# Block-causal attention and a feed-forward on one core: V loaded in f32 and cast on GpSimd, weights in pieces, a full last key block, and attention of batch b placed among the feed-forward of batch b-2

## The chip, the cores and the metric

The kernel runs on one core of a Trainium2 chip. A core has TensorE (PE in the profile; PEld is its weight load), VectorE (DVE), ScalarE (ACT), GpSimd (POOL) and SyncE (SP), each with an instruction stream of its own that runs in the order in which it was written; they meet through semaphores. Sixteen DMA engines move data between HBM and SBUF. The metric is the device time of one execution in microseconds (us); lower is better.

## The reference

Eight batches of eight heads, 576 positions of 64 elements. Attention is block-causal in blocks of 64, and its output, with the heads side by side, is the input of a feed-forward with the gate h * sigmoid(beta * h):

```python
scores = np.matmul(q, k.transpose(0, 1, 3, 2)) / np.sqrt(64)     # (8, 8, 576, 576)
scores = np.where(block_i >= block_j, scores, -1e9)              # block = position // 64
attn = np.exp(scores - scores.max(-1)); attn /= attn.sum(-1) + 1e-9
x = np.matmul(attn, v).transpose(0, 2, 1, 3).reshape(4608, 512)
h = x @ w_in                                                     # 512 -> 2048
g = h * (1.0 / (1.0 + np.exp(-beta * h)))
out = g @ w_out                                                  # 2048 -> 512, float32
```

## The kernel before

**Attention units.** The work of attention is cut into 32 units u = 4b + c, one for batch b and head pair c. Each unit goes through these steps:

- Q and K of the pair are loaded in f32 by one DMA each on SP (L396) into one of four buffers, and cast to bf16 (L402), on DVE for units 0 to 3 and on POOL after that.
- PE transposes them, six matmuls each (L408); DVE copies the result to QT and KT (L416).
- PE makes the scores in four groups g0 (L437). The contraction is over 64 rows, and the two heads of the pair use the two halves of the array. ACT takes the exponential of the three large groups (L444) into E and of the last key block, 64 keys, into F (L456). POOL clears the masked corners of E (L450, L452).
- AV (L482): for each head and each block i of 128 queries, PE multiplies the key blocks t = 0 to i of E by V, 15 matmuls a head, 30 a unit. V has a column of ones as its 65th, so the sum of the exponentials comes out beside the product. Query block 4 has only 64 queries and key block 4 only 64 keys, so its weights are 64 columns wide, and for t = 4 the contraction is over 64 rows: head h lies in rows 64h to 64h + 63 of F and of V's fifth block.
- DVE takes the reciprocal of the sums (L493) and multiplies (L501); PE transposes the result (L510), and DVE copies it into xT (L516), the input of the feed-forward.

V of a batch is loaded by six DMAs on POOL (L370, L374), which cast to bf16 on the way, into one of two buffers Vn; batch 0 in two halves of four heads.

**Feed-forward chunks.** Nine chunks r of 512 rows. First half: for j = 0 to 15, four matmuls with w_in (L531), tanh on ACT (L539) and the product on DVE into gT (L543; the sigmoid is written through tanh, with the factor one half applied to beta and to the output). Second half: for w = 0 to 3, sixteen matmuls with w_out (L551), a copy with the factor one half (L560) on ACT or DVE, and the store on SP (L566). Chunk r needs the attention of every batch that its rows touch: chunk 0 needs batch 0, chunk 1 batches 0 and 1.

**Weights.** w_in and w_out are loaded on POOL with a cast to bf16, in four operations of four DMAs each (L345, L351).

**What sets the order.** Every operation is entered in a planner (`Plan`, L40) with the engines that may run it, an assumed duration and latency, its dependencies, the buffers ("tiles") that it needs, and a priority `prio`. `schedule` (L68) plays the program through with these numbers. Whenever an engine is free it takes the ready operation with the lowest prio, and for a tile the slot that is free. The result is a fixed order on each engine, written out by `emit` (L246) with semaphore waits in front of each operation. At run time the order doesn't change: an operation that waits holds all that stand behind it on its engine. PSUM has eight banks; 0 to 3 serve the scores in pairs (class "PP") while scores are still to come, 4 to 7 all the rest ("P1").

Before the change attention of unit u has prio 10u to 10u + 5 on PE, and feed-forward chunk r has 1000 + 100r and up. So attention always goes first, and the feed-forward takes what is left:

```python
o = P.op("PE", 6 * 57, ft, ..., prio=10 * u)                                    # transposes
av = P.op("PE", 30 * 57 + 300, fav, ..., mode="full", prio=10 * u + 4)          # AV
o = P.op("PE", 4 * mm(512), fh, ..., mode="full", prio=1000 + 100 * r + j)      # feed-forward
```

Of the kernel before, what the change touches and what calls it, by code (L numbers as in the profile page):

```python
# [6 lines left out]
f32 = mybir.dt.float32  # L7
# [21 lines left out]
class Op:  # L29
    def __init__(self, engs, dur, lat, emit, deps, tiles, prio, mode, dma):  # L30
        self.engs, self.dur, self.lat, self.emit = engs, dur, lat, emit
        self.deps, self.tiles, self.prio, self.mode, self.dma = list(deps), tiles, prio, mode, dma
        self.eng = None
        self.start = self.end = None
        self.order = None
        self.need = False
        self.tick = None


class Plan:  # L40
# [17 lines left out]
    def op(self, engs, dur, emit, deps=(), tiles=(), prio=0, lat=None, mode=None, dma=None):  # L58
        engs = (engs,) if isinstance(engs, str) else tuple(engs)
        o = Op(engs, dur, dur if lat is None else lat, emit, deps, list(tiles), prio, mode, dma)  # L60
# [7 lines left out]
    def schedule(self):  # L68
# [18 lines left out]
        now, done, nsched = 0.0, 0, 0  # L87
# [21 lines left out]
        while nsched < len(self.ops) or pend:  # L109
# [25 lines left out]
            while progress:  # L135
                progress = False
                for e in engs:
# [48 lines left out]
                    o.eng, o.start, o.end = e, start, start + o.lat  # L186
                    eng_free[e] = start + o.dur
# [79 lines left out]
def bass_blockwise_causal_attn__then__act_swish_beta_kernel(  # L267
# [10 lines left out]
    with es:  # L278
# [7 lines left out]
        Ks = [sb(f"Ks{i}", [96, 2, 6, 64], f32) for i in range(NS)]  # L286
        Qn = [sb(f"Qn{i}", [96, 6, 2, 64], bf16) for i in range(NQ)]
# [4 lines left out]
        E3 = [sb(f"E{i}", [128, 3, 2, 512], bf16) for i in range(NE)]  # L292
        E4 = [sb(f"F{i}", [128, 64], bf16) for i in range(NE)]
# [16 lines left out]
        for c, n in (("Qs", NS), ("Ks", NS), ("Q", NQ), ("K", NQ), ("V", NQ), ("QT", 3), ("KT", 3), ("E", NE), ("inv", 3), ("xq", 2),  # L310
                     ("th", 3), ("gT", 2), ("ost", 3)):
            P.slots(c, n)
# [9 lines left out]


        def mk(fn):
# [11 lines left out]
        ones = [P.op("POOL", 200, mk(lambda g, i=i: g.memset(Vn[i][:, :, :, 64:65], 1.0)), prio=-5)  # L336
                for i in range(NQ)]
# [3 lines left out]
                  lat=2500, dma=("d_beta", 1), prio=-5)  # L341
        win = []
        for a in range(4):
            def f(g, e, a=a):
                return [g.dma_start(w_in[:, c, 512 * a:512 * (a + 1)],  # L345
                                    moe_w_in[128 * c:128 * (c + 1), 512 * a:512 * (a + 1)]) for c in range(4)]
            win.append(P.op("POOL", 2200, f, lat=9000, dma=(f"d_win{a}", 4), prio=40 + a))
        wout = []
        for a in range(4):
            def f(g, e, a=a):  # L350
                return [g.dma_start(w_out[:, j, :], moe_w_out[128 * j:128 * (j + 1), :])  # L351
                        for j in range(4 * a, 4 * a + 4)]
            wout.append(P.op("POOL", 2200, f, lat=9000, dma=(f"d_wout{a}", 4), prio=44 + a))
# [8 lines left out]
        load = {}  # L362
        tl = {}
        for b in range(B):
            t = tl[b] = P.tile("V")
            for h0, h1 in ([(0, 4), (4, 8)] if b == 0 else [(0, 8)]):
                def fv(g, e, t=t, b=b, h0=h0, h1=h1):
                    z = []
                    for i in range(4):
                        z.append(g.dma_start(  # L370
                            Vn[t.slot][:, i, h0:h1, 0:64],
                            v[b, h0:h1, 128 * i:128 * i + 128, :].rearrange("h p d -> p h d")))
                    for o in range(2):
                        z.append(g.dma_start(  # L374
                            Vn[t.slot][64 * o:64 * o + 64, 4, h0 + o:h1:2, 0:64],
# [3 lines left out]
                c = 6 * (500 + 70 * (h1 - h0))  # L379
                o = P.op("POOL", c, fv, deps=ones, tiles=[t], lat=c + 3000, prio=20 if b == 0 else 50 + b,  # L380
                         dma=["d_V", h0, 6])
# [5 lines left out]
        for u in range(NU):  # L387
# [4 lines left out]
            for nm, td, src, raw_, nat, dst in (("Q", tq, q, Qs, Qn, QT), ("K", tk, k, Ks, Kn, KT)):  # L392
# [6 lines left out]
                o = P.op("SP", 500, fl, tiles=[ts], lat=4000, prio=u, dma=["d_" + nm, 0, 1])  # L399
# [6 lines left out]
                def ft(g, e, tn=tn, pt=pt, nat=nat):  # L406
                    for i in range(6):
# [5 lines left out]
                         prio=10 * u)  # L413
# [9 lines left out]
            for g0 in range(4):  # L423
                ps = P.tile("PP" if g0 < 3 else "P1")

                def fq(g, e, ps=ps, g0=g0, tq=tq, tk=tk):
                    blocks = {0: [(0, 0, 512, 0)], 1: [(1, 128, 576, 0), (0, 512, 576, 448)],
                              2: [(2, 256, 576, 0), (3, 384, 576, 320)], 3: [(4, 512, 576, 0)]}[g0]
                    for t, q0, q1, off in blocks:
                        m = min(128, 576 - 128 * t)  # L430
                        for h in range(2):
# [9 lines left out]
                         lat=(220 if g0 < 3 else 60) + 200, mode="row", prio=10 * u + 1 + (g0 >= 2))  # L441
# [19 lines left out]
            def eblk(te, t, i, h):  # L461
                w = 128 if i < 4 else 64
                if t == 4:
                    return E4[te.slot][64 * h:64 * h + 64, 0:64]
                g0, off = {0: (0, 0), 1: (1, 0), 2: (2, 0), 3: (2, 320)}[t]
                if t == 0 and i == 4:
                    a = E3[te.slot][:, 1, h, 448:512]
                    return bass.AP(a.tensor, a.offset, [a.ap[0], [1, 128]])
                a = off + 128 * i - 128 * t
                return E3[te.slot][:, g0, h, a:a + w]  # L470

# [3 lines left out]
            def fav(g, e, te=te, pa=pa, pb=pb, Tv=Tv, c=c):  # L475
                for h in range(2):
                    for i in range(5):
                        for t in range(i + 1):
                            m = 64 if i == 4 and t else 128
                            o = PS[0:m, (pa if h == 0 else pb).slot, 65 * i:65 * i + 65]  # L480
                            r = slice(64 * h, 64 * h + 64) if t == 4 else slice(0, 128)
                            z = g.matmul(o, eblk(te, t, i, h), Vn[Tv.slot][r, t, 2 * c + h, 0:65],  # L482
                                         start=(t == 0), stop=(t == i or (i == 4 and t == 0)),
                                         skip_group_check=(i == 4))
                return z

            av = P.op("PE", 30 * 57 + 300, fav, deps=ex + zs + [load[u]], tiles=[te, Tv, pa, pb, ti, tx],
                      lat=30 * 57 + 500, mode="full", prio=10 * u + 4)
# [150 lines left out]
```

## Time and profile before

| | us |
|---|---|
| median of 3 runs | 418.41 (418.2 to 418.69) |
| the profiled execution | 415.65 |
| its span, first to last instruction | 413.8 |
| ACT busy | 215.2 (52%) |
| DVE busy | 195.7 (47%) |
| POOL busy | 129.6 (31%) |

The span is what the engines' records cover; the profiled execution is a little longer than it, and the median of the runs a little longer again. "Busy" is the time in which at least one instruction of an engine runs. Matmuls overlap in PE's pipeline, so the busy time of one matmul is longer than the distance from its start to the next one's start. In the windows view a row gives a stretch, its length, the busy time and the count of instructions (x) of PE, PEld, DVE, ACT and POOL, then the granted clock, the share of the DMA engines' time, and GB/s; asked for one line of the kernel, it gives the engines of that line alone. In the timeline a row gives the start, the busy time, the engine, the line, the operation and the count; what stands in brackets is the idle time before it and what ended it.

### The profile page before, as it was taken

What the parts mean: (1) busy time and instruction counts of PE and PEld (TensorE: products, weight loads), DVE (VectorE), ACT (ScalarE), POOL (GpSimd) and SP (SyncE); (2) the same over time, 40 slices, a digit from 0 to 9 for tenths busy, and PEclk for the clock granted to TensorE, in tenths of its full rate; (3) what the DMA queues carried; (4) which work ended last, traced back from release to release, by engine and by line L of the source; (5) the groups of instructions that cost most, each with busy time, mean ns of one, the idle gap of its engine ahead of it and who ended that gap; (6) DMA issues with size and microseconds to landing.
All of it is one profiled execution on the core that took longest, in us unless ns stands there. A gap on an engine that the chain in (4) does not pass through costs nothing.

```text
span 413.8 us, 7477 instructions
## 1 busy us (share of the span) xinstructions
PE 379.6 (92%) x3006; PEld 201.5 (49%) x3041; DVE 195.7 (47%) x377; ACT 215.2 (52%) x309; POOL 129.6 (31%) x248
## 2 busy tenths in 40 slices
PE   2359998999999998999999999999999999999986
PEld 1136643565655665455555444444444444444432
DVE  2515567244768776683337407137054071370520
ACT  1143676236786766943485437256174272461721
POOL 8366789226678967930010000000000000000000
PEclk9999999999999999999999999999999999999999
DMA  7998999939497999900100020110100101101001
GB/s 179 253 224 174 191 220 187 96 109 141 121 140 205 158 136 202 78 2 27 53 25 2 27 77 0 53 51 2 76 26 27 76 0 52 51 2 76 25 28 76
DMA packets 60899, 37.73 MB, mean 91 GB/s; under 512 B 39856, under 2 KB 56256, under 8 KB 60864
## 3 DMA queue, kind: packets, MB, share of 16 engines
q0 software_dynamic: 42336, 8.92, 24.9%
q1 hardware_dynamic: 18528, 28.33, 23.2%
q8 instruction: 24, 0.39, 0.4%
q14 instruction: 11, 0.09, 0.1%
HBM read 36.71 MB, written 9.44 MB: 112 GB/s over the span
## 4 chain that ended last, share of the span: by engine, by line
PE 74%; ACT 10%; DMA 6%; DVE 4%; POOL 3%; issue 2%; POOLq 0%
PE PS L551 30%; PE PS L531 25%; PE PS L482 11%; ACT E L444 8%; DMA Vn<-in_v_dram 5%; PE PS L437 4%; PE PS L408 2%; PE PS L510 2%; ACT th L539 2%; DMA w_out<-in_moe_w_out_dram 2%; DVE xq L501 1%; POOL w_out L351 1%; DVE gT L543 1%; POOL Vn L370 1%; DVE QT L416 1%
## 5 line engine op out<-in xcount | busy, mean ns | idle before, releaser
L543 DVE SCALAR_TENSOR_TENSOR gT<-th,PS 128x512 bf16<-128x512 f32 x144 | 98.6, 687 | 118.2 <-ACT th L539 118.1
L531 PE MATMUL PS<-xT,w_in 128*128 128x512 bf16 x557 | 127.2, 381 | 2.8 <-DVE KT L416 0.9
L444 ACT ACTIVATE E<-PS 128x1024 bf16<-128x1024 f32 x96 | 94.8, 1034 | 67.1 <-PE PS L437 66.9
L551 PE MATMUL PS<-w_out,gT 128*128 128x512 bf16 x560 | 124.8, 379 | 4.8 <-issue 1.5
L539 ACT ACTIVATE th<-PS,beta 128x512 f32<-128x512 f32 x144 | 99.3, 693 | 27.9 <-PE PS L531 27.9
L551 PEld LDWEIGHTS PS<-w_out,gT 128*128 128x128 bf16 x576 | 55.7, 98 | 70.5 <-issue 2.0
L531 PEld LDWEIGHTS PS<-xT,w_in 128*128 128x128 bf16 x576 | 54.7, 98 | 66.7 <-issue 2.0
L560 ACT ACTIVATE ost<-PS 128x512 f32<-128x512 f32 x36 | 21.5, 597 | 100.4 <-PE PS L551 100.4
L482 PE MATMUL PS<-Vn,E 128*128 128x65 bf16 (+1 forms) x896 | 48.8, 202 | 5.4 <-DMA Vn<-in_v_dram 3.8
L482 PEld LDWEIGHTS PS<-Vn,E 128*128 128x128 bf16 (+1 forms) x896 | 38.4, 104 | 16.0 <-issue 5.4
L437 PE MATMUL PS<-QT,KT 64*128 64x64 bf16 (+5 forms) x384 | 41.6, 310 | 2.2 <-ACT E L444 1.4
L370 POOL DMA_DIRECT2D Vn<-in_v_dram x36 | 31.2, 905 | 7.5 <-PE PS L482 6.5
L450 POOL MEMSET E<- 64x128 bf16 x64 | 13.2, 206 | 54.0 <-ACT E L444 49.2
L501 DVE TENSOR_TENSOR xq<-PS,inv 128x320 bf16<-128x320 f32 x64 | 29.3, 486 | 0.0
L416 DVE COPY QT<-PS 128x576 bf16<-128x576 bf16 x32 | 24.1, 752 | 6.4 <-PE PS L408 5.9
L516 DVE COPY xT<-PS 128x576 bf16<-128x576 bf16 x32 | 14.5, 453 | 26.2 <-PE PS L510 26.1
L402 POOL CAST Qn<-Qs 96x768 bf16<-96x768 f32 x28 | 23.1, 824 | 9.7 <-PE PS L408 8.1
L493 DVE RECIPROCAL inv<-PS 128x5 f32<-128x5 f32 x64 | 8.4, 173 | 36.3 <-PE PS L482 35.9
L437 PEld LDWEIGHTS PS<-QT,KT 64*128 64x128 bf16 (+1 forms) x384 | 14.9, 100 | 21.0 <-issue 7.3
L416 DVE COPY KT<-PS 128x576 bf16<-128x576 bf16 x32 | 24.0, 750 | 1.9 <-PE PS L408 1.7
L402 POOL CAST Kn<-Ks 96x768 bf16<-96x768 f32 x28 | 23.1, 824 | 1.8
L408 PE MATMUL PS<-identB,Kn 96*128 96x96 bf16 x192 | 15.8, 227 | 7.8 <-DVE KT L416 4.6
(27 smaller groups left out, 142.9 us busy)
## 6 DMA issues: line engine op xcount, KB each, us to landing
Qs<-in_q_dram SPq DMA_DIRECT2D x32, 288.0 KB, 4.4
Ks<-in_k_dram SPq DMA_DIRECT2D x32, 288.0 KB, 4.5
out_dram<-ost SPq DMA_DIRECT2D x36, 256.0 KB, 2.0
Vn<-in_v_dram POOLq DMA_DIRECT2D x28, 128.0 KB, 4.1
w_in<-in_moe_w_in_dram POOLq DMA_DIRECT2D x16, 128.0 KB, 6.9
w_out<-in_moe_w_out_dram POOLq DMA_DIRECT2D x16, 128.0 KB, 5.0
Vn<-in_v_dram POOLq DMA_DIRECT2D x8, 64.0 KB, 16.9
Vn<-in_v_dram POOLq DMA_DIRECT2D x14, 32.0 KB, 3.3
```

Source lines behind the costliest of these rows:

```text
L370: z.append(g.dma_start(Vn[t.slot][:, i, h0:h1, 0:64], v[b, h0:h1, 128 * i:128 * i + 128, :].rearrange("h p d -> p h d")))
L402: return g.tensor_copy(nat[tn.slot][:], raw_[ts.slot][:].rearrange("p h j d -> p j h d"))
L408: z = g.transpose(PSb[:, pt.slot, 96 * i:96 * i + 96], nat[tn.slot][:, i, :, :].rearrange("p h d -> p (h d)"), identB[0:96, 0:96])
L416: return g.tensor_copy(dst[td.slot][:].rearrange("c (p j) -> c p j", j=6), PSb[:, pt.slot, 0:576].rearrange("c (j p) -> c p j", j=6))
L437: z = g.matmul(o, KT[tk.slot][r, 128 * t:128 * t + m], QT[tq.slot][r, q0:q1])
L444: return g.activation(E3[te.slot][:, g0, :, :], PS[:, ps.slot:ps.slot + 2, :], ACT.Exp, scale=0.125)
L482: z = g.matmul(o, eblk(te, t, i, h), Vn[Tv.slot][r, t, 2 * c + h, 0:65], start=(t == 0), stop=(t == i or (i == 4 and t == 0)), skip_group_ ...
L501: return g.tensor_tensor(xq[tx.slot][:, :, 64 * w:64 * w + 64], a, x, ALU.mult)
L531: z = g.matmul(PS[:, ph.slot, :], w_in[:, c, 128 * j:128 * j + 128], xT[:, c, row:row + RC], start=(c == 0), stop=(c == 3))
L539: return g.activation(th[tt.slot][:], PS[:, ph.slot, :], ACT.Tanh, scale=beta[:, j:j + 1])
L543: return g.scalar_tensor_tensor(out=gT[tg.slot][:, j, :], in0=th[tt.slot][:], scalar=1.0, in1=PS[:, ph.slot, :], op0=ALU.add, op1=ALU.mult)
L551: z = g.matmul(PS[:, po.slot, :], gT[tg.slot][:, j, 128 * w:128 * w + 128], w_out[:, j, :], start=(j == 0), stop=(j == NJ - 1))
```

## The change

Five things are changed together.

1. **Full last key block.** E and F of a slot become one tensor Ef of 3200 columns: F is its columns 3072 to 3135, and 64 columns of zeros follow. The weights of each AV matmul are 128 columns and 128 rows, also for query block 4 and key block 4. For t = 4 the rows of the other head meet zeros in V's fifth block, ones column included. Output rows 64 to 127 of query block 4 are not used.
2. **V in f32.** V's six DMAs a batch go to SP and write f32 to a buffer Vs; POOL casts it into Vn in one instruction (two for batch 0, which is split into heads 0, 1 and heads 2 to 7). Memsets at the start clear the unused parts.
3. **Weights in pieces.** Each weight DMA is an operation of its own. w_in's pieces wait for Q and K of unit 3, w_out's for those of unit 6. The loads of Q, K and V for units 4 to 7 wait for w_in's second quarter, those from unit 8 on for w_out's third. A feed-forward step waits for the pieces that it reads; in chunk 0 the second half is cut into parts of four j for w = 0 to 2.
4. **Pacing.** From batch 2 on the attention of batch b has the priorities of feed-forward chunk b-2: its units come at 994, 998.9, 1003.8 and 1008.7 plus 100(b-2), the chunk's steps at 1000 to 1019 plus 100(b-2).
5. **The planner's numbers.** Loads and stores take turns on one modelled DMA resource (`rings`, `xfer`) in place of a fixed latency each, and AV's assumed duration is 30 x 46 ns.

```diff
+                    if o.dma is not None:
+                        rings = max(rings, start + 700) + o.xfer
+                        o.end = rings + 1500
...
+        Vs = [sb(f"Vs{i}", [128, 5, 8, 64], f32) for i in range(NQ)]
...
-        E3 = [sb(f"E{i}", [128, 3, 2, 512], bf16) for i in range(NE)]
-        E4 = [sb(f"F{i}", [128, 64], bf16) for i in range(NE)]
+        Ef = [sb(f"E{i}", [128, 3200], bf16) for i in range(NE)]
+        E3 = [e[:, 0:3072].rearrange("p (c h n) -> p c h n", c=3, h=2) for e in Ef]
+        E4 = [e[:, 3072:3136] for e in Ef]
...
+        LAG = 2
+        def pr(u):
+            b, c = divmod(u, NPAIR)
+            return 10 * u if b < 2 else 994 + 100 * (b - LAG) + 4.9 * c
...
-            win.append(P.op("POOL", 2200, f, lat=9000, dma=(f"d_win{a}", 4), prio=40 + a))
+                win.append(P.op("POOL", 650, fwi, xfer=880, dma=(f"d_win{a}", 1), prio=-19))
...
-            wout.append(P.op("POOL", 2200, f, lat=9000, dma=(f"d_wout{a}", 4), prio=44 + a))
+            wout.append(P.op("POOL", 650, fwo, xfer=880, dma=(f"d_wout{j // 4}", 1), prio=-18))
...
-            for h0, h1 in ([(0, 4), (4, 8)] if b == 0 else [(0, 8)]):
+            for h0, h1 in ([(0, 2), (2, 8)] if b == 0 else [(0, 8)]):
...
-                            Vn[t.slot][:, i, h0:h1, 0:64],
+                            Vs[ts.slot][:, i, h0:h1, :],
                             v[b, h0:h1, 128 * i:128 * i + 128, :].rearrange("h p d -> p h d")))
...
-                o = P.op("POOL", c, fv, deps=ones, tiles=[t], lat=c + 3000, prio=20 if b == 0 else 50 + b,
-                         dma=["d_V", h0, 6])
+                o = ld["V", b, h0] = P.op("SP", 6 * 400, fv, deps=vzero, tiles=[ts], xfer=5000 * n,
+                         prio=(0.5 if h0 == 0 else 2.5) if b == 0 else 4 * b + 0.5 - 3 * (b > 1), dma=["d_V", h0, 6])
+                def fw(g, e, ts=ts, t=t, h0=h0, h1=h1):
+                    return g.tensor_copy(Vn[t.slot][:, :, h0:h1, 0:64], Vs[ts.slot][:, :, h0:h1, :])
+                o = P.op("POOL", 300 + 2140 * n, fw, deps=[o, *ones], tiles=[ts, t],
+                         prio=4 * b + (0.5 if h0 == 0 else 1))
...
                 if t == 4:
-                    return E4[te.slot][64 * h:64 * h + 64, 0:64]
+                    a = 3072
...
-                return E3[te.slot][:, g0, h, a:a + w]
+                return Ef[te.slot][:, a:a + 128]
...
-                            m = 64 if i == 4 and t else 128
-                            o = PS[0:m, (pa if h == 0 else pb).slot, 65 * i:65 * i + 65]
-                            r = slice(64 * h, 64 * h + 64) if t == 4 else slice(0, 128)
-                            z = g.matmul(o, eblk(te, t, i, h), Vn[Tv.slot][r, t, 2 * c + h, 0:65],
+                            o = PS[:, (pa if h == 0 else pb).slot, 65 * i:65 * i + 65]
+                            z = g.matmul(o, eblk(te, t, i, h), Vn[Tv.slot][:, t, 2 * c + h, 0:65],
...
+        for w in win:
+            w.deps += [ld["Q", 3], ld["K", 3]]
+        for w in wout:
+            w.deps += [ld["Q", 6], ld["K", 6]]
+        for u in range(4, NU):
+            w = win[4:8] if u < 8 else wout[8:12]
+            for o in [ld["Q", u], ld["K", u]] + ([ld["V", u // 4, 0]] if u % 4 == 0 else []):
+                o.deps += w
...
+                parts = [(0, NJ)] if r or w > 2 else [(4 * a, 4 * a + 4) for a in range(4)]
...
-                o = P.op("PE", 16 * mm(512), fo, deps=gs + wout, tiles=[po, tg], lat=16 * mm(512) + 170,
-                         mode="full", prio=1000 + 100 * r + 16 + w)
+                    o = P.op("PE", n * mm(512), fo, deps=gs[j0:j1] + wout[j0:j1] + ([o] if o else []),
+                             tiles=[po, tg], lat=n * mm(512) + 170, mode="full",
+                             prio=1000 + 100 * r + 16 + (w if n == NJ else 0.01 * j0 + 0.001 * w))
```

100 lines of the change are left out of this document (56 added, 44 removed).

## The prediction

> **What bounds the kernel now.** First I read the page's totals and its 40 slices, then four stretches of the windows view.
>
> ```profile
> PE 379.6 (92%) x3006; PEld 201.5 (49%) x3041; DVE 195.7 (47%) x377; ACT 215.2 (52%) x309; POOL 129.6 (31%) x248
> PE   2359998999999998999999999999999999999986
> 0.00:55.00 55.00, 35.23 (x328) 21.86 (x329) 24.01 (x47) 20.80 (x27) 36.07 (x74) 1.00 1.09 205
> 55.00:84.00 29.00, 27.07 (x204) 13.77 (x204) 15.19 (x28) 16.08 (x24) 19.31 (x32) 1.00 1.21 156
> 84.00:222.00 138.00, 131.03 (x1629) 81.28 (x1642) 83.59 (x196) 89.79 (x126) 74.22 (x143) 1.00 0.63 105
> 222.00:413.80 191.80, 186.30 (x852) 84.58 (x869) 72.94 (x107) 88.57 (x133) 0.00 (x0) 1.00 0.10 39
> ```
>
> From 55 us on TensorE (PE) is the bound: 344.4 of 358.8 us busy, idle 1.9 + 7.0 + 5.5 = 14.4. There, time falls only if PE gets less to do. Before 55 us it waits or creeps. The chain of waits and the timeline say for what:
>
> ```profile
> 8.51 19.82 DMA Vn<-in_v_dram
> ...
> 273.54 10.74 PE PS L531 x49
> 17.54 0.75 DVE L416 COPY KT<-PS 128x576 bf16<-128x576 bf16 x1
> 18.34 0.66 PE L408 MATMUL PS<-identB,Kn 96*128 96x96 bf16 x6 [4.57 <-DVE KT L416]
> 54.09 1.49 PE L531 MATMUL PS<-xT,w_in 128*128 128x512 bf16 x3 [0.33 <-issue]
> L531 PE MATMUL PS<-xT,w_in 128*128 128x512 bf16 x557 | 127.2, 381 | 2.8 <-DVE KT L416 0.9
> ```
>
> The first V lands only at 28.3 us; the first scores came late too, since KT's copy stood on DVE behind all eight casts of pairs 0 to 3. The feed-forward starts at 54.09. One of its matmuls lasts 381 ns, overlapping the next; start to start it takes (10.74 - 0.38)/48 = 0.2158 us, so all 1152 take **248.6 us**, which the change does not touch.
>
> **Price of one attention unit (a head pair), warm.** Between 84 and 222 us the weight loads of the lines L408, L437, L482, L510, L531 and L551 are, in this order (the second count of each row):
>
> ```profile
> 84.00:222.00 138.00, 15.83 (x264) 12.09 (x264) 1.00 0.63 105
> 84.00:222.00 138.00, 27.74 (x290) 10.73 (x290) 1.00 0.63 105
> 84.00:222.00 138.00, 42.35 (x772) 34.15 (x769) 1.00 0.63 105
> 84.00:222.00 138.00, 13.13 (x125) 8.69 (x125) 1.00 0.63 105
> 84.00:222.00 138.00, 21.88 (x88) 8.09 (x98) 1.00 0.63 105
> 84.00:222.00 138.00, 20.40 (x90) 8.92 (x96) 1.00 0.63 105
> ```
>
> Feed-forward: 194 x 0.2158 = 41.9 us of the 131.03 busy. The other 89.2 us are 264/12, 290/12, 769/30 and 125/5 units of the four steps, 24.2 on average: **3.69 us a unit**. Check: by 55 us some 5.6 units' worth and 4 feed-forward matmuls were done, so 55 + 247.7 + 26.4 x 3.69 + 14.4 = 414.5, against 413.8.
>
> **The change, part by part.**
>
> **1. Full last key block.** L482 now multiplies one head by 11 matmuls of 128x128, three of 128x64 and one of 64x64:
>
> ```profile
> 143.37 0.51 PE L482 MATMUL PS<-Vn,E 128*128 128x65 bf16 x11
> 143.81 0.28 PE L482 MATMUL PS<-Vn,E 128*64 128x65 bf16 x3
> 144.02 0.21 PE L482 MATMUL PS<-Vn,F 64*64 64x65 bf16 x1
> 144.16 0.51 PE L482 MATMUL PS<-Vn,E 128*128 128x65 bf16 x11
> ```
>
> Head to head: 144.16 - 143.37 = 0.79 us. The eleven start 0.03 us apart ((0.51 - 0.21)/10, 0.21 being one alone); at each change of shape the next start is 0.12 to 0.15 us later (144.02 to 144.16, for one). After the change all 15 have one shape: 0.45 us a head, 0.34 saved, **0.67 us a unit**: 3.69 becomes 3.02. Bounds: nothing, if a long run cannot hold 0.03 us; 0.35 a head at best. I take the row's own spacing, since eleven in a row hold it in both heads.
> [...]
>
> **2. V in f32 on SP's queue, cast on POOL.** Six SP issues a batch replace six on POOL, four of them of 905 ns (L370).
>
> ```profile
> q0 software_dynamic: 42336, 8.92, 24.9%
> q1 hardware_dynamic: 18528, 28.33, 23.2%
> L370 POOL DMA_DIRECT2D Vn<-in_v_dram x36 | 31.2, 905 | 7.5 <-PE PS L482 6.5
> L402 POOL CAST Qn<-Qs 96x768 bf16<-96x768 f32 x28 | 23.1, 824 | 9.7 <-PE PS L408 8.1
> L444 ACT ACTIVATE E<-PS 128x1024 bf16<-128x1024 f32 x96 | 94.8, 1034 | 67.1 <-PE PS L437 66.9
> L450 POOL MEMSET E<- 64x128 bf16 x64 | 13.2, 206 | 54.0 <-ACT E L444 49.2
> ```
>
> The cast: 2560 elements a partition against 768 in 824 ns gives 2.75 us, against 3.6 us for four of the six issues alone: POOL gains. In steady state both hide under PE; without that cover a batch would wait 2.75 us once, for the first unit's AV. A V packet in the hardware queue is not shown. Mean packet time is 0.249 x 16 x 413.8/42336 = 39 ns in q0, mostly V, and 83 ns in q1, of 1.5 and 2 KB. A batch has 8 x 576 = 4608 packets on 16 engines: 11 us or 24 us. I take the lower: it is the same 256 B read, and without a cast in the queue.
>
> **3. Order of loads, weights in pieces.** Weights now wait for Q3 and K3, so batch 0 has the DMA to itself.
>
> ```profile
> 0.00:10.00 10.00, 2.27 (x19) 1.53 (x19) 2.98 (x5) 1.28 (x1) 8.91 (x22) 1.00 0.75 176
> 10.00:20.00 10.00, 2.98 (x28) 1.74 (x28) 5.16 (x9) 0.41 (x1) 3.79 (x5) 1.00 1.25 255
> 17.07 0.56 DVE L402 CAST Kn<-Ks 96x768 bf16<-96x768 f32 x1 [0.77 <-DMA Ks<-in_k_dram]
> w_in<-in_moe_w_in_dram POOLq DMA_DIRECT2D x16, 128.0 KB, 6.9
> L351 POOL DMA_DIRECT2D w_out<-in_moe_w_out_dram x16 | 8.5, 555 | 0.0
> ```
>
> By 17.07 us the queues had moved 1.76 + 7.07 x 0.255 = 3.56 MB. Batch 0 needs 8 x 0.295 + 1.18 = 3.54 MB, so K3 lands at 17 again, with V beside it. The first two heads' V is issued behind Q0 and K0 and lands well before their exps end; the first AV then starts about 12 us (Q0's chain and three exps of 1034 ns) instead of 28.5. In that stage PE is slow:
>
> ```profile
> 28.47 0.76 PE L482 MATMUL PS<-Vn,E 128*128 128x65 bf16 x11 [3.85 <-DMA Vn<-in_v_dram]
> 48.17 1.23 PE L437 MATMUL PS<-QT,KT 64*128 64x320 bf16 x8
> 49.33 0.66 PE L408 MATMUL PS<-identB,Qn 96*128 96x96 bf16 x6
> ...
> 50.40 0.61 PE L437 MATMUL PS<-QT,KT 64*128 64x448 bf16 x4
> 50.94 0.77 PE L510 MATMUL PS<-identB,xq 128*128 128x128 bf16 x5
> 51.49 0.49 PE L437 MATMUL PS<-QT,KT 64*128 64x320 bf16 x2
> 139.83 0.43 PE L408 MATMUL PS<-identB,Qn 96*128 96x96 bf16 x6
> ```
>
> Six transposes take 0.66 us here and 0.43 at 139.83, though the granted clock reads 1.00 in both rows. Start to start a unit takes 1.16 + 1.07 + 0.54 + 0.55, and AV after the change 30 x (0.76 - 0.21)/10 = 1.65: 5.0 us. Four units are 19.9 us, of which 3.9 (two units' Q and K transposes and the first scores) lie before 12: attention of batch 0 ends near 28, and the **first feed-forward matmul comes at 29 us** (K3's cast, transposes, copy, scores, three exps, AV and output transposes alone would allow 27).
> w_in's first quarter, waiting on K3, is there by then: 1.05 MB at 255 GB/s after 17 is 4.1 us, and such a DMA took 6.9 us to land. SP's own waits, for w_in's second and w_out's third quarter, hold only later loads: no output is due yet. Then DMA must bring 4.2 + 3.5 + 4.2 MB, 47 us at 255 and 58 at 205 GB/s (0 to 55 us), until 64 to 75 us. PE has for it 13.8 (first half of chunk 0) + 12.1 (batch 1) + 13.8 (chunk 1), and chunk 0's second half as pieces of w_out land. Two places leave gaps: POOL issues sixteen w_out pieces (16 x 555 ns, 9 us) ahead of the casts of pairs 6 and 7, queued behind their wait for Q6 and K6; and PE's fixed order waits where a landing is late. I allow **6 us**; bounds 0 and 18 (both POOL runs of 9 us uncovered).
>
> **4. Pacing.** It moves attention, it removes no instruction. PE was 95% busy in the mixed stage already, so I take the old idle: 7.0 + 5.5 = **12.5 us**; the 1.9 are in the allowance. Bounds: 7 us better (idle gone), or the stall of the slower rival below.
>
> **The sum.** 29 + 248.6 + 28 x 3.02 (84.6) + 6 + 12.5 = **380.7 us** of span. The profiled run took 415.65 us with 413.8 of span, 1.85 beside it, and the median 418.41 is 2.76 above that: 380.7 + 4.6 = **385.3 us**.
>
> **The rivals.**
> - **AV keeps its mean spacing** of 42.35/772 = 55 ns, a limit of issue and not of shape: 28 x 0.67 = 19 us come back, 404. For: no run longer than 11 was seen. Against: the gaps sit at the changes of shape. 7%.
> - **V packets cost 83 ns**, and SP, which runs in order, holds Q and K behind them: batches 0 and 1 come 13 us later each, part of it covered: 393 to 412. For: a queue shared by small and large packets. Against: q0's 39 ns. 15%.
> - **A better ramp or mix**: idle in the mixed stage goes (7 us) or PE turns fast earlier. 368 to 378, 12%. [...]
> - **Slower: the paced order makes each AV wait.** If the fixed order puts each unit's AV directly behind its last exp, PE stands for an exp and a memset, 1.034 + 0.2 us, in each of 28 units: 35 us, 420. It decides from 1.18 us a unit (33 us). Against: feed-forward matmuls are at hand to stand between, and a unit had only 7.0/24.2 = 0.29 us of idle in the mixed stage. 4%.
> - **The change doesn't do what it says**: the feed-forward still starts past 45 us, as PE's order holds it behind batch 1. Only part 1 is left, 21 us: 397. 6%.
>
> **The numbers.** Forecast 56% (377 to 393); the rivals as above. The range takes in the better ramp and the shorter shortfalls: **371 to 404**; some 2 in 10 lie outside. A difference of 0.2% (0.8 us) is about what a measurement here can tell from none: faster 0.95, same 0.01, slower 0.04.
>
> **What would show it.** L482 in one shape, at 0.03 us, 0.9 us a unit; the first L531 near 29 us with w_in's landing ahead of it; a V landing before 10 us; POOL casts of 2.75 us; PE idle below 14 us after 55 us. I am wrong if L531 starts after 40, if the chain of waits shows exps or POOL between 60 and 260 us, or if AV in the stretches still takes 50 ns a matmul.

## The result, and the profile after

| | before | changed |
|---|---|---|
| median of 4 runs each | 418.31 us (416.26 to 418.69) | 397.82 us (396.45 to 399.86) |
| profiled execution, its span | 415.65, 413.8 us | 396.65, 394.8 us |

The ratio is 0.9524, 95% interval 0.9465 to 0.9582: 20.5 us faster. The forecast was 385.3 us; the time is 12.5 us above it and within the range of 371 to 404. The span is 394.8 us where 380.7 was forecast, and these 14.1 us are what has to be explained. Of the runs below, one execution (the profiled one with half of the exps) was 1.5% slower than the fastest of its kernel, at a lower clock, and its ratio leaves that one out.

First the page of the changed kernel: the totals, PE's 40 slices with the granted clock, and two groups of its lists.

```profile
PE 360.2 (91%) x2993; PEld 184.6 (47%) x3041; DVE 192.6 (49%) x380; ACT 209.3 (53%) x308; POOL 108.2 (27%) x212
...
PE   3876999959899999999999999999999999999986
...
PEclk9997999989999999999999999999999999999999
...
q1 hardware_dynamic: 56256, 37.77, 37.3%
...
L507 PE MATMUL PS<-Vn,E 128*128 128x65 bf16 x960 | 36.5, 198 | 2.5 <-POOL E L480 1.5
```

PE is still the bound: it lost 19.4 us of work (379.6 to 360.2) and the span 19.0. AV, all 960 matmuls, is busy for 36.5 us. The slices are full from about 40 us on, apart from one dip near 80 us, and now the clock row shows dips as well.

Next, four stretches of the windows view of the changed kernel, cut at its first feed-forward matmul (33.05 us) and at the end of attention (294 us).

```profile
0.00:33.05 33.05, 19.89 (x238) 13.26 (x240) 17.47 (x39) 13.49 (x17) 17.59 (x49) 0.93 0.88 163
33.05:84.00 50.95, 44.07 (x396) 22.71 (x402) 25.38 (x49) 25.41 (x38) 28.47 (x44) 0.97 1.06 217
84.00:294.00 210.00, 200.51 (x1926) 105.34 (x1956) 116.08 (x243) 128.06 (x192) 62.12 (x120) 0.99 0.40 103
294.00:394.80 100.80, 95.73 (x436) 43.28 (x444) 33.63 (x50) 42.33 (x64) 0.00 (x0) 1.00 0.11 42
```

They settle the sum term by term. When the feed-forward starts, attention of batch 0 is complete, so 28 units are left, as forecast. From 33.05 us on PE is busy 44.07 + 200.51 + 95.73 = 340.31 us; without the feed-forward's 248.6 that is 91.7 us, or **3.28 us a unit**.

| term | forecast | measured | difference |
|---|---|---|---|
| first feed-forward matmul | 29 | 33.05 | +4.05 |
| 28 units of attention | 84.6 (3.02 each) | 91.7 (3.28 each) | +7.1 |
| idle, ramp (33 to 84 us) | 6 | 6.88 | +0.9 |
| idle, mixed stage (84 to 294 us) | 7.0 | 9.49 | +2.5 |
| idle, after attention | 5.5 | 5.07 | -0.4 |
| span | 380.7 | 394.8 | +14.1 |

**AV**, in the timeline of PE after (two units side by side):

```profile
242.24 1.08 PE L507 MATMUL PS<-Vn,E 128*128 128x65 bf16 x30
243.49 1.08 PE L507 MATMUL PS<-Vn,E 128*128 128x65 bf16 x30 [0.17 <-DVE gT L576]
244.50 0.39 PE L465 MATMUL PS<-QT,KT 64*128 64x448 bf16 x4
```

All 30 have one shape. From 243.49 to the next group's start they take 1.01 us: 0.034 us each, for both heads, where before one head alone took 0.79.

**The ramp**, in the same timeline view:

```profile
14.24 1.83 PE L507 MATMUL PS<-Vn,E 128*128 128x65 bf16 x30
...
28.42 1.69 PE L507 MATMUL PS<-Vn,E 128*128 128x65 bf16 x30 [1.46 <-POOL E L480]
31.32 0.77 PE L534 MATMUL PS<-identB,xq 128*128 128x128 bf16 x5 [1.21 <-DVE xq L525]
33.05 2.86 PE L564 MATMUL PS<-xT,w_in 128*128 128x512 bf16 x7 [0.95 <-DVE xT L540]
37.42 0.43 PE L436 MATMUL PS<-identB,Qn 96*128 96x96 bf16 x6 [1.51 <-POOL Qn L430]
```

The first AV comes at 14.24 us, where 12 was forecast and 28.5 was the row before. No DMA holds it: V's first cast was over at 7.5 us, and the last exp's clear at 12.7. Its bracket is empty; it stands in PE's order behind transposes and scores of later units. The last steps of batch 0 then wait in a chain with nothing between them in PE's order, 1.46 + 1.21 + 0.95 us, for an exp's clear, a normalization and a copy. That is the late start.

**SP's queue and a store.** Timeline after, SP's issues (SPq), ACT and PE around 70 to 83 us:

```profile
69.46 5.67 SPq L392 DMA_DIRECT2D Vs<-in_v_dram  x4
75.17 1.82 SPq L396 DMA_DIRECT2D Vs<-in_v_dram  x2
77.04 0.60 SPq L605 DMA_DIRECT2D out_dram<-ost  x1
81.69 0.60 ACT L599 ACTIVATE ost<-PS 128x512 f32<-128x512 f32 x1 [7.38 <-DMA out_dram<-ost]
82.34 0.25 PE L465 MATMUL PS<-QT,KT 64*64 64x64 bf16 x4 [3.28 <-ACT ost L599]
```

SP is held 7.5 us by six issues of one batch's V. A store stands behind them and then takes 4.6 us to land (the median store takes 2.0), so a buffer of ACT comes free late, ACT waits 7.38 us, and PE 3.28 us behind ACT: the dip near 80 us, and half of the ramp's 6.88 us of idle.

### The profile page after: what moved, and what is told of

Read it like the earlier page. It is cut to its first block, busy times and chain, and to the rows that moved or that the text cites. A ratio compares the mean times of both kernels' runs of the same rounds, so it can differ in the third digit from the quotient of the medians.

```text
span 394.8 us, 7420 instructions
## 1 busy us (share of the span) xinstructions
PE 360.2 (91%) x2993; PEld 184.6 (47%) x3041; DVE 192.6 (49%) x380; ACT 209.3 (53%) x308; POOL 108.2 (27%) x212
## 2 busy tenths in 40 slices
DMA packets 60898, 42.44 MB, mean 107 GB/s; under 512 B 39856, under 2 KB 56256, under 8 KB 60864
## 3 DMA queue, kind: packets, MB, share of 16 engines
q1 hardware_dynamic: 56256, 37.77, 37.3%
## 4 chain that ended last, share of the span: by engine, by line
PE 60%; ACT 16%; DVE 7%; DMA 6%; SPq 6%; issue 3%; POOL 2%; POOLq 0%
PE PS L588 31%; PE PS L564 19%; ACT E L472 8%; ACT th L572 6%; PE PS L507 5%; SPq L392 4%; DVE gT L576 3%; PE PS L465 2%; DVE xq L525 2%; PE PS L436 2%; DMA Ks<-in_k_dram 1%; DMA Qs<-in_q_dram 1%; PE PS L534 1%; DMA w_in<-in_moe_w_in_dram 1%; DMA out_dram<-ost 1%
## 5 line engine op out<-in xcount | busy, mean ns | idle before, releaser
L564 PE MATMUL PS<-xT,w_in 128*128 128x512 bf16 x543 | 133.4, 384 | 5.6 <-issue 1.7
L472 ACT ACTIVATE E<-PS 128x1024 bf16<-128x1024 f32 x96 | 97.2, 1057 | 28.0 <-PE PS L465 27.7
L564 PEld LDWEIGHTS PS<-xT,w_in 128*128 128x128 bf16 x576 | 51.0, 98 | 61.7 <-issue 4.6
L599 ACT ACTIVATE ost<-PS 128x512 f32<-128x512 f32 x35 | 20.9, 598 | 105.4 <-PE PS L588 98.0
L465 PE MATMUL PS<-QT,KT 64*64 64x64 bf16 (+5 forms) x384 | 40.3, 295 | 6.1 <-ACT ost L599 3.3
L507 PE MATMUL PS<-Vn,E 128*128 128x65 bf16 x960 | 36.5, 198 | 2.5 <-POOL E L480 1.5
L507 PEld LDWEIGHTS PS<-Vn,E 128*128 128x128 bf16 x960 | 33.4, 100 | 9.7 <-issue 2.5
L525 DVE TENSOR_TENSOR xq<-PS,inv 128x320 bf16<-128x320 f32 x64 | 28.6, 486 | 0.0
L406 POOL CAST Vn<-Vs 128x2560 bf16<-128x2560 f32 (+2 forms) x9 | 18.7, 2083 | 21.4 <-DMA Vs<-in_v_dram 14.2
L436 PE MATMUL PS<-identB,Qn 96*128 96x96 bf16 x192 | 14.7, 217 | 10.7 <-POOL Vn L354 4.6
L534 PE MATMUL PS<-identB,xq 128*128 128x128 bf16 (+1 forms) x160 | 17.2, 220 | 1.7 <-DVE xq L525 1.7
```

The source lines that it names most:

```text
L436: z = g.transpose(PSb[:, pt.slot, 96 * i:96 * i + 96], nat[tn.slot][:, i, :, :].rearrange("p h d -> p (h d)"), identB[0:96, 0:96])
L465: z = g.matmul(o, KT[tk.slot][r, 128 * t:128 * t + m], QT[tq.slot][r, q0:q1])
L472: return g.activation(E3[te.slot][:, g0, :, :], PS[:, ps.slot:ps.slot + 2, :], ACT.Exp, scale=0.125)
L507: z = g.matmul(o, eblk(te, t, i, h), Vn[Tv.slot][:, t, 2 * c + h, 0:65], start=(t == 0), stop=(t == i))
L525: return g.tensor_tensor(xq[tx.slot][:, :, 64 * w:64 * w + 64], a, x, ALU.mult)
L534: z = g.transpose(PSb[:, px.slot, 128 * i:128 * i + r], xq[tx.slot][0:r, i, :], identB[0:r, 0:r])
```

## The experiments

Each run is compared with the kernel before on the same chip; the bracket is the 95% interval of the ratio. The kernel before varied between chips (medians 415.35 to 418.31 us), so ratios are compared, not times. Two theories stood against each other at the start: that the missing 14 us are waits, at SP's queue above all, and that PE itself has more to do than the sum allowed. With them went the question which part brings how much.

**Full block alone.** The kernel before, with part 1 only:

```diff
-                    return E4[te.slot][64 * h:64 * h + 64, 0:64]
+                    a = 3072
...
-                return E3[te.slot][:, g0, h, a:a + w]
+                return Ef[te.slot][:, a:a + 128]
```

> The kernel before with the full last key block alone. If the changes of shape cost what the rows show (0.67 us a unit, PE being the bound from 55 us on), 27 to 28 units give 18 to 21 us: near 399 against 418. If a long run of AV matmuls can't hold 0.03 us, or if what PE saves turns into waits for ACT, the time stays above 410.

404.07 us against 416.69, ratio 0.9698 (0.9634 to 0.9762). Its windows row from 84 us to the end of attention:

```profile
84.00:209.00 125.00, 114.15 (x1556) 68.70 (x1553) 80.50 (x190) 87.40 (x122) 72.24 (x139) 0.99 0.68 109
```

It gains 12.6 us where the steps priced part 1 at 21 (32 units at 0.67). PE idles 10.85 of 125 us; before it idled 7.0 of 138. Part of the time that AV saves becomes waiting; the likely reason, argued and not shown, is that the next step of attention is not ready where little feed-forward is mixed in. The chain of waits of that stretch names ACT's exps with 28.7%, and 23.3% in the same view of the kernel before (84 to 222 us).

The gain is not all made there. Six transposes, the first feed-forward matmul, and from the kernel before six transposes, in PE's timelines:

```profile
32.35 0.66 PE L417 MATMUL PS<-identB,Qn 96*128 96x96 bf16 x6
...
34.11 0.43 PE L417 MATMUL PS<-identB,Kn 96*128 96x96 bf16 x6
...
46.61 1.91 PE L536 MATMUL PS<-xT,w_in 128*128 128x512 bf16 x4
```

```profile
57.47 0.42 PE L408 MATMUL PS<-identB,Qn 96*128 96x96 bf16 x6
```

With the full block six transposes take 0.66 us at 32.35 and 0.43 at 34.11, so PE is at full speed from about 33 us on, apart from spells (clock 0.50 from 39.8 to 50 us); before, they still took 0.68 us at 52.53 and 0.42 only at 57.47. The feed-forward starts at 46.61 instead of 54.09, after the same attention work: 7.5 us of the 12.6, where four shorter AVs were priced at 2.7.

**No pacing.** The changed kernel, attention always first:

```diff
-            return 10 * u if b < 2 else 994 + 100 * (b - LAG) + 4.9 * c
+            return 10 * u
```

> The changed kernel with attention's old priorities (10u for every unit). If the pacing is worth nothing, as the prediction has it, the time stays within 3 us of 397.8. If the paced order is what costs the 2.5 us by which a chunk is longer than forecast (42.2 against 39.7 us), it falls by 5 to 15 us; if the pacing carries the change, it rises by over 5 us.

404.36 us against 416.69, 0.9704 (0.9662 to 0.9746). Windows, a stretch of the ramp and attention from 84 us to its end:

```profile
28.00:36.00 8.00, 6.09 (x43) 3.13 (x43) 2.26 (x6) 0.69 (x1) 1.69 (x4) 0.50 1.17 202
84.00:192.00 108.00, 96.69 (x1451) 59.55 (x1450) 75.61 (x179) 80.93 (x112) 63.59 (x121) 0.94 0.72 169
```

The first feed-forward matmul starts at 32.52 us, as early as in the changed kernel, and the whole gains no more than the full block alone. The loads' early start is lost again: PE idles 11.31 of 108 us, and the clock is granted at 0.94 on average, with spells at 0.50; the first row is another one.

**Old shapes of AV in the changed kernel.** The plan and its order stay, AV's matmuls are the old ones:

```diff
-                    a = 3072
+                    return Ef[te.slot][64 * h:64 * h + 64, 3072:3136]
...
-                            o = PS[:, (pa if h == 0 else pb).slot, 65 * i:65 * i + 65]
+                            m = 64 if i == 4 and t else 128
+                            o = PS[0:m, (pa if h == 0 else pb).slot, 65 * i:65 * i + 65]
```

> The changed kernel with AV's old shapes, in the changed kernel's order. By the changed kernel's rows a unit's AV falls from 1.65 to 1.04 us: 28 units are 17 us, so near 415. If the order leaves PE idle so that AV's length is hidden, it stays below 405.

410.66 us against 416.69, 0.9856 (0.9796 to 0.9917). Page (AV) and windows:

```profile
L510 PE MATMUL PS<-Vn,E 128*128 128x65 bf16 (+2 forms) x960 | 56.4, 204 | 3.4 <-issue 2.3
```

```profile
84.00:294.00 210.00, 204.68 (x1801) 106.85 (x1802) 106.19 (x218) 119.98 (x181) 61.40 (x116) 0.98 0.41 106
```

AV is busy 56.4 us, against 36.5: 19.9 us, near the 21 that the steps gave to part 1. The spans differ by 410.3 - 394.8 = 15.5. Not all of that is shapes at full clock: PE comes to full speed only at about 40 us here (eight feed-forward matmuls take 3.59 us from 36.32 and 1.73 from 40.24), against 22 in the changed kernel (six transposes take 0.66 us at 19.41 and 0.43 at 22.02), and the feed-forward starts at 36.32 us, 3.3 later. PE's idle time between 84 and 294 us is 5.32 us with the old shapes and 9.49 with the new ones: 4.2 us of the saving turn into waits.

**V's loads issued by POOL**, so that SP is free for Q, K and the stores; POOL issued V before the change as well:

```diff
-                o = ld["V", b, h0] = P.op("SP", 6 * 400, fv, ...
+                o = ld["V", b, h0] = P.op("POOL", 6 * 800, fv, ...
```

> The changed kernel with V's f32 loads issued on POOL in place of SP, cast as before. If SP, held 5 to 10 us by each batch of V issues, is what keeps loads and stores late between 33 and 126 us, the time falls by 5 to 10 us. If the DMA engines themselves are the limit there, or POOL's own work is delayed instead, it stays or rises.

406.19 us against 416.69, 0.9765 (0.9694 to 0.9836): worse than the changed kernel. Timeline of PE:

```profile
26.15 1.83 PE L507 MATMUL PS<-Vn,E 128*128 128x65 bf16 x30 [8.49 <-POOL Vn L406]
...
48.21 1.89 PE L564 MATMUL PS<-xT,w_in 128*128 128x512 bf16 x4
```

PE stands 8.49 us for POOL's first cast of V, and the feed-forward starts at 48.2. This moves the late ramp onto POOL; whether SP's queue costs anything net it does not tell. It bounds what the early start is worth: 15.2 us later cost, with all else that the edit moves, 2.4% ± 0.9, some 10 us.

**Stores issued by POOL**, to take them from behind V's issues:

```diff
-            P.op("SP", 400, fd, deps=[x] ...
+            P.op("POOL", 600, fd, deps=[x] ...
```

> The changed kernel with the output stores issued on POOL in place of SP. If the first store, which stood behind a batch of V on SP, cost the 5 us that PE waits at 78 us, the time falls by 3 to 5 us. If that wait only hides another (K and Q of the next pairs, also late on SP), it stays within 2 us.

405.58 us against 417.73, 0.9721 (0.9641 to 0.9801). The page's row of ACT's copies names no store any more:

```profile
L599 ACT ACTIVATE ost<-PS 128x512 f32<-128x512 f32 x35 | 20.9, 597 | 101.1 <-PE PS L588 101.1
```

And its windows row for the ramp:

```profile
33.00:84.00 51.00, 46.74 (x407) 23.44 (x405) 25.43 (x49) 26.20 (x40) 27.57 (x46) 0.94 1.04 215
```

The wait is gone, and PE's idle time in the ramp falls from 6.88 us to 4.26 (51.00 - 46.74). Yet the time rises. So the store's wait is real, and removing it in this way gains nothing; the plan is drawn anew, and other waits (3.44 us up to 39.12 us for a cast of Q on POOL) and a lower clock (0.94 in this row, 0.97 in the changed kernel's) stand in its place.

**Four variations of the plan.** Slower loads told to the planner (V's issue 7200 ns in place of 2400, all transfers longer); units spaced by 7.5 in place of 4.9; V of the later batches behind Q and K; loads of units 4 to 7 waiting for w_in's first quarter instead of its second:

```diff
-                o = ld["V", b, h0] = P.op("SP", 6 * 400, ..., xfer=5000 * n,
+                o = ld["V", b, h0] = P.op("SP", 6 * 1200, ..., xfer=6000 * n,
...
-            return 10 * u if b < 2 else 994 + 100 * (b - LAG) + 4.9 * c
+            return 10 * u if b < 2 else 994 + 100 * (b - LAG) + 7.5 * c
...
-                         prio=... 4 * b + 0.5 - 3 * (b > 1) ...
+                         prio=... 4 * b + 0.5 ...
...
-            w = win[4:8] if u < 8 else wout[8:12]
+            w = win[0:4] if u < 8 else wout[8:12]
```

> The changed kernel, the planner told of slower loads: Q and K 1350 ns, V 6000, a weight piece 1050 on the DMA resource, 7200 ns of SP per batch of V. If the fixed order loses time before 126 us because loads land later than planned, the time falls by 3 to 8 us. If the DMA is simply the limit there, the order of the waits changes and the time stays within 2 us.

> The changed kernel with the four units of a batch 7.5 apart in priority in place of 4.9, so that the last one falls among the second half of its chunk. If the exps, bunched beside the tanhs of the first half, are what makes a unit cost 3.6 us in the mixed stage, the 28 units gain 0.1 to 0.3 us each: 3 to 8 us. If a unit's price is that of its shapes on PE, the time stays within 2 us.

> The changed kernel with V of batches 2 to 7 given a priority three pairs later on SP, beside its own batch's first pair. If V, loaded early, keeps Q and K of the nearer pairs late between 60 and 126 us, the stretch from 84 to 126 us gives 2 to 5 us. If the DMA is only needed later there, or the fixed order drawn anew costs as much, the time stays within 3 us or rises.

> The changed kernel with the loads of pairs 4 to 7 waiting for w_in's first quarter in place of its second. If batch 1's late loads hold PE between 33 and 55 us, Q4 lands some 4 us earlier and the time falls by 2 to 4 us. If w_in's later quarters then come as much later and hold the feed-forward, it stays within 2 us or rises.

In this order: 401.38 us (0.9619, 0.9559 to 0.9679), 400.37 (0.9588, 0.9523 to 0.9652), 400.58 (0.9632, 0.9587 to 0.9676), 401.86 (0.9668, 0.9608 to 0.9728). None beats the changed kernel's 0.9524; the second can't be told from it. The first, whose plan knows SP's delays best, starts the feed-forward at 34.39 us and the last at 38.66. A wait at SP that a better plan could simply remove did not show up; that is evidence against the theory of waits, not a proof, since each of these edits redraws the order of every engine, and the granted clock changed with it (means of 0.966 to 0.983, against 0.986).

**Half of the exps left out.** The changed kernel, same plan and order; from batch 2 on each of the three large exps of a unit covers only half of its columns, and the other half of E keeps old values:

```diff
-                        return g.activation(E3[te.slot][:, g0, :, :], PS[:, ps.slot:ps.slot + 2, :], ACT.Exp,
+                        return g.activation(E3[te.slot][:, g0, :, 0:n], PS[:, ps.slot:ps.slot + 2, 0:n], ACT.Exp,
```

> The changed kernel, same order on every engine, with the three large exps of each unit from batch 2 on over half of their columns (the other half of the scores keeps old values of E). Each chunk of 42.2 us has 14 us in which ACT is busy 97%. If ACT sets the pace there, a chunk falls by 1.5 to 4 us and six chunks by 9 to 20. If a unit's price is PE's own (its shapes and the changes between them), ACT only idles more and the time falls by less than 4 us.

399.15 us against 415.35, 0.9556 (0.948 to 0.9631): no gain. The time as a whole says little, since the clock from 84 to 126 us was granted at 0.84 against 0.97. Windows from 126 to 294 us, where both run at full clock, first the changed kernel:

```profile
126.00:294.00 168.00, 161.95 (x1443) 82.91 (x1465) 85.23 (x178) 95.92 (x145) 38.80 (x76) 1.00 0.24 69
```

and then with half exps:

```profile
126.00:294.00 168.00, 162.06 (x1437) 83.38 (x1460) 87.85 (x179) 79.30 (x146) 41.59 (x80) 1.00 0.27 75
```

ACT has 16.6 us less to do; PE's busy and idle times stay within 0.2 us, and it gets as much done: 16.0 units and 510 feed-forward matmuls in the first row, 16.0 and 514 in the second, by their weight loads. In the paced stage the length of the exps does not set the time. For the largest term that speaks for the second theory; the tanhs, and DVE behind them, were not shortened.

**The other corners.** Parts 2, 3 and 5 alone (old shapes, no pacing), and parts 1 and 4 on the old loads:

```diff
-            return 10 * u if b < 2 else 994 + 100 * (b - LAG) + 4.9 * c
+            return 10 * u
...
-                return Ef[te.slot][:, a:a + 128]
+                return E3[te.slot][:, g0, h, a:a + w]
```

```diff
+        def pr(u):
+            b, c = divmod(u, NPAIR)
+            return 10 * u if b < 2 else 994 + 100 * (b - LAG) + 4.9 * c
...
-            av = P.op("PE", 30 * 57 + 300, fav, ..., prio=10 * u + 4)
+            av = P.op("PE", 30 * 46, fav, ..., prio=pr(u) + .4)
```

> The changed kernel without pacing and with AV's old shapes: only the loads (V in f32, weights in pieces, the order of loads) differ from the kernel before. By the prediction's sum the earlier start alone is worth some 15 us: near 402. If what starts earlier waits later, for exps or for loads, it stays above 410.

> The kernel before with the full last key block and the pacing, but V, the weights and the order of loads as they were. If the earlier start (first feed-forward matmul at 33 in place of 54 us) is worth what it gave without the other two parts, 6 us, the time is near 404. If the loads carry more than half of the forecast's 25 us of earlier start, it is above 408; if what starts earlier only waits later, it is near 398.

411.35 us against 417.73, 0.9875 (0.9799 to 0.9952), and 402.23 against 416.98, 0.9651 (0.9586 to 0.9716). The corners that were run, with the gain in per cent and half the width of its interval (pacing alone was not run):

| full block | loads | pacing | gain |
|---|---|---|---|
| yes | | | 3.0 ± 0.6 |
| | yes | | 1.3 ± 0.8 |
| yes | yes | | 3.0 ± 0.4 |
| | yes | yes | 1.4 ± 0.6 |
| yes | | yes | 3.5 ± 0.7 |
| yes | yes | yes | 4.8 ± 0.6 |

Read from the last row: without the full block 3.3% (14 us) are gone, without pacing 1.8% (7.5 us), without the loads 1.3% (5.3 us; with these intervals just told from nothing). These sum to 6.4%, more than the whole: the parts lean on each other. The loads add nothing to the full block until pacing is there too, and pacing adds nothing that can be told to the loads while AV keeps its old shapes. With the full block and pacing on the old loads the feed-forward starts at 44.46 us already, so of the 21 us of earlier start the loads bring 11.4.

## Why the prediction was right, and where it was off

**1. The full block: right, with help that the step did not foresee.** AV's 19.9 us over 32 units are 0.62 a unit, against 0.67. The rival that AV keeps 55 ns a matmul fell. What the step left out is that PE's saved time has to meet ready work: taking the full block away costs 14 us. It also left out the clock. With the full block PE came to full speed earlier than with the old shapes, in one profiled execution each: at about 33 us against 57 on the old loads, at 22 us, and without pacing by 23.2 (AV in 1.08 us there), against 40 on the new ones. How much of the 14 us this is no run separates, and why full speed comes earlier with the full block is not shown.

**2. V in the hardware queue: right in direction, and the packets cheaper still.** q1's mean is now 0.373 x 16 x 394.8/56256 = 41.9 ns. If the 19392 packets that are not V's kept the 83 ns of before, V's 36864 took about 20 ns each (an estimate), under the 39 of the forecast. POOL's cast is cheaper too, 2.32 us for 2.75 (its row by form, changed kernel):

```profile
L406 POOL CAST Vn<-Vs 128x2560 bf16<-128x2560 f32 x7 | 16.2, 2319 | 18.7 <-DMA Vs<-in_v_dram 11.5 <-PE PS L507 7.1
```

The rival "V packets cost 83 ns" fell by its price; its second half came true in another form. SP is held in its own issues, with a store behind them: in the first 30 us an issue of V on L392 took 0.47 us in the median (0.42 to 3.42), and four from 69.46 us on took 1.4 each. Why some take so long is not shown. The step "SP's own waits hold only later loads" had looked at waits alone.

**3. The ramp: right but 4 us late.** 33.05 for 29. The step counted the units' work at PE's slow pace and let a chain of waits bound it at 27; PE was busy 19.89 us up to there, the 19.9 that were counted, and the waits at the end of batch 0 (3.6 us) stand on top of that work. That the work came out is in part luck: PE was fast from 22 to 28.6 us (AV in 1.08 us at 23.58) and slow again after that (1.69 at 28.42). The allowance of 6 us of gaps measured 6.88, though one of its two places, POOL's issues, was not the one that cost most: the store was. A start 21 us earlier than before was also never worth 21 us. The sum knew this, since before its start the old kernel had done 5.6 units and the new one 4; the 10 us for 15 of V's loads on POOL agree.

**4. Pacing: the idle nearly right, its reason wrong.** 9.49 + 5.07 = 14.6 us for 12.5. But that pacing brings nothing, as the sum had it, was wrong for this kernel: without it the kernel is 7.5 us slower. From 84 us to attention's end a unit, waits included, costs (108 - 68 x 0.2158)/23.2 = 4.02 us without pacing and (210 - 578 x 0.2158)/23.2 = 3.68 with it (68 and 578 are the feed-forward's weight loads there): 8 us over 23.2 units. Idle is the smaller share, 0.49 us a unit against 0.41, so 1.8 us. The clock can be the larger one: granted at 0.94 it takes (an estimate) up to 0.06 x 108 = 6.5 us from that stretch, against 0.01 x 210 = 2.1 paced. That pacing adds only 0.5% to the full block on the old loads, where the unpaced clock was 0.99, fits this. No run separates the two. They may be one thing: without pacing the clock read 0.62 from 85.0 to 88.4 us and 0.64 from 112.2 to 115.6, each time right after a row in which PE waited (busy 0.45 and 1.65 of 3.4 us).

**5. The price of a unit: the step that failed, +7.1 us.** 3.02 was 3.69 less AV's saving, with every feed-forward matmul charged 0.2158 us. From the distances between starts in PE's timeline (idle in brackets taken off, matmuls counted by their weight loads) come, before (84 to 222 us) and after (84 to 294):

| us | before | after |
|---|---|---|
| transposes of Q, K | 0.70 a unit | 0.80 a unit |
| scores | 1.08 | 1.11 |
| AV | 1.62 | 1.00 |
| output transposes | 0.41 | 0.43 |
| one feed-forward matmul | 0.204 | 0.216 |

Before, a unit came with 194/24.2 = 8 feed-forward matmuls, each 0.012 us under its charge, so 0.1 us of attention's price was hidden in them. After, it comes with 578/23.2 = 25, which take their full charge. With the transposes' 0.10, the scores' 0.03, the output transposes' 0.02 and the 0.05 that AV fell short, 0.3 us a unit are found, beside the 0.26 of the first account (the two draw the line between busy and idle a little differently). The half clock is little of it: from 126 to 294 us, at full clock, a unit still costs (161.95 - 510 x 0.2158)/16.0 = 3.24.

The old shapes in the changed kernel's order show where part of it comes from. Their row for the same stretch:

```profile
126.00:294.00 168.00, 165.43 (x1356) 83.56 (x1355) 80.13 (x160) 91.38 (x141) 40.91 (x77) 1.00 0.26 73
```

With 497 feed-forward matmuls and 14.67 units in it, a unit costs 3.97, where the old order had 3.69. So in the new order the full block takes off 0.73, and the order itself adds 0.28, which the sum did not have.

Why it adds that is open. PE changes from one line to another 190 times for 23.2 units, 8.2 a unit, where it was 143 for 24.2, 5.9. That each change costs something, as the changes of shape inside AV did (0.12 to 0.15 us), fits the paced kernels. It does not explain the full block alone, where PE changed no more often (138 for 23.2) and a unit still took 3.25 us by the same account: (114.15 - 180 x 0.2158)/23.2. Short waits that the busy time hides are a second candidate. One place, from the timeline after:

```profile
228.83 1.29 DVE L576 SCALAR_TENSOR_TENSOR gT<-th,PS 128x512 bf16<-128x512 f32 x2 [15.62 <-ACT th L572]
229.68 0.42 PE L436 MATMUL PS<-identB,Kn 96*128 96x96 bf16 x6
230.17 0.55 PEld L564 LDWEIGHTS PS<-xT,w_in 128*128 128x128 bf16 x4 [0.22 <-DVE gT L576]
230.18 1.04 PE L564 MATMUL PS<-xT,w_in 128*128 128x512 bf16 x4
```

From six transposes to the feed-forward's next matmul it is 0.50 us, where the group of six before them took 0.25 (229.43 to 229.68). The weight load waited for DVE, whose product was done at 230.12, and PE's row shows no idle time. From 126 to 294 us weight loads wait 8.0 us for this product, 0.5 us a unit; before (84 to 222 us) it was 2.0 us, 0.08 a unit. What PE itself loses by it is less, and not known. With half of the exps a unit still cost 3.19. So the mis-sized term is known, 3.28 us for 3.02, and that it is not waiting for long exps is shown; how much is PE's own work and how much short waiting stays open.

**The other rivals.** AV directly behind its exp: AV waited 2.5 us in all, not 35. "It doesn't do what it says": the start came at 33, and not past 45. One sign of being wrong that the prediction named did come: from 60 to 260 us the chain of waits names exps, with 12.0%. The half exps show that a share in the chain was no price here. A faster clock in the ramp came and went, as the windows after show:

```profile
25.20:28.60 3.40, 1.18 (x18) 0.66 (x18) 1.08 (x3) 2.80 (x4) 3.23 (x9) 1.00 1.13 150
79.80:83.20 3.40, 0.25 (x4) 0.14 (x4) 0.00 (x0) 1.51 (x3) 2.08 (x1) 1.00 0.92 261
...
22.00:28.60 6.60, 3.79 (x68) 2.50 (x65) 3.53 (x10) 4.00 (x5) 5.58 (x14) 1.00 1.11 149
28.60:35.40 6.80, 4.63 (x41) 2.81 (x39) 1.69 (x6) 0.69 (x1) 1.47 (x3) 0.50 1.13 198
35.40:42.00 6.60, 5.09 (x36) 2.21 (x34) 4.42 (x7) 3.14 (x5) 1.65 (x2) 1.00 1.23 225
...
83.20:86.60 3.40, 3.34 (x16) 1.11 (x16) 0.00 (x0) 2.94 (x7) 3.09 (x6) 0.50 1.11 283
```

PE turned fast at about 22 us (six transposes in 0.66 us at 19.41, 0.43 at 22.02), where before it was slow still at 50 (0.66, the rows in the prediction), and slow again from 28.6 to 35.4, clock 0.50, over the chain that ends the ramp. What PE turning fast earlier is worth by itself, a part of this rival's 368 to 378, no run shows; with fast and slow stretches in it, PE was busy 19.89 us up to 33.05, where the sum had 19.9. Both spells at 0.50 come right after a stretch with little work on PE: busy 1.18 and 0.25 of 3.4 us, the first two rows.

## What to carry to other kernels

Price a step in the mixture in which it will run: with the old shapes the new order alone made a unit 0.28 us dearer, and the unit's price was half of the miss. (That the mixture is not the whole reason, the full block alone shows.) Work taken off the bounding engine pays only as far as its next work is ready: 19.9 us of AV brought 14, part of which may be the clock, and the early loads brought nothing to the full block until the order of the work was changed too. What an engine does before a late start isn't lost, so a start moved forward by 21 us is worth much less than 21.

## What the runs showed of the hardware

- In the changed kernel 30 matmuls of one tile shape and 65 columns took 0.034 us each, at a granted clock of 1.00 (243.49 to 244.50 us). In a spell granted at 0.50 (39.8 to 50 us with the full block alone) the busy time of 30 of them was 1.83 us instead of 1.08.
- The granted clock read 0.50 for 6.8 us (28.6 to 35.4) and for 3.4 us (83.2 to 86.6) in the changed kernel; without pacing one spell lasted 17 us (24.4 to 41.5). In the changed kernel both came right after 3.4 us in which PE was busy 1.18 and 0.25 us. Within the second PE was busy 3.34 of 3.4 us and the clock still 0.50. No rule is worked out: without pacing a fall came after a row with 1.60 busy of 3.4 us (20.4 to 23.8), and in the changed kernel rows with 1.98 (36.0 to 39.4) and 2.00 (105.4 to 108.8) were followed by 1.00.
- The row of the clock read 1.00 also where PE was slow: in the changed kernel it reads 1.00 up to 28.6 us, and AV took 1.83 us at 14.24 and 1.08 at 23.58. In the profiled runs PE became fast at about 57 us before, 33 with the full block alone, 40 with the old shapes on the new loads, and 22 in the changed kernel, by the transposes and matmuls named above.
- Four issues of V's loads held SP 5.67 us, in front of a store that took 0.60; two more held it 1.82 us.
